# One small maximum moved from the last chunk of a weight-generation loop to behind the last lags

## The chip, the cores and the metric

The kernel runs on one core of a Trainium2 chip. A core has five engines with a queue each: PE (TensorE, matrix products, with its weight loads shown as PEld), DVE (VectorE), ACT (ScalarE), POOL (GpSimd) and SP (SyncE, which here issues most DMAs). The metric is the device time of one execution in microseconds; lower is better. An engine works through its queue in order and waits for other engines by semaphores.

## The reference

Four layers are applied to x of shape (1, 2048, 512): S4 convolution, SwiGLU FFN, and both again with the same weights. Each adds its result to x and starts from a layer norm of x.

```
def A(u):                      # S4
    logdA = exp(log_dt)[:, None] * (A_re + 1j * A_im)          # (512, 128)
    K = einsum("dn,dnl,dn->dl", C, exp(logdA * l), dt * B).real  # 512 kernels of length 2048
    return irfft(rfft(pad(u)) * rfft(pad(K))) + u * Dskip      # causal convolution
def B(x):                      # F = 1376
    return (silu(x @ w_gate) * (x @ w_up)) @ w_down
x = x + A(layernorm(x)); x = x + B(layernorm(x))
x = x + A(layernorm(x)); x = x + B(layernorm(x))
```

## The kernel before, in words

**The generation of the convolution kernels.** The 512 channels are worked through in eight chunks of 64 (`DC`, `NCH`). For each chunk DVE, ACT and POOL build tables of powers (`gen_exp`, `gen_turns`, `gen_trig`, `gen_g` at L454 to L487, `gen_e` at L439 to L452); PE multiplies them into the kernel's lags (`lags`, L489 to L498); ACT copies the lags out (`spread_in`, L507); they are spread over the partitions by DMA, or for the last two chunks by PE (`spread_pe`, L518 to L525); the skip weight is added (`skip`, L503); and PE transforms them to spectra (`spectra`, products in L531, copies in L554 to L559, one sum in L563).

**The scales of the FFN's weights.** The FFN multiplies in fp16, with each weight split into a high and a low half. The scales of the split come from bounds on the weights: `norms` (L314 to L340) loads `w_down`, `w_gate` and `w_up` piece by piece in 43 units and five groups. A unit's ACT instruction squares the piece (L333), and a PE product with a matrix of ones adds the squares of each column into the group's PSUM tile `nrm` (L336). When a group is complete, DVE takes the maximum over its columns (`largest`, L339) into the group's column of `cmx`. `scales` (L342 to L356) makes the maximum of `cmx` (L344) and ten tiny DVE steps of bit arithmetic into `sc6`. ACT needs `sc6` for the first high halves (L664), DVE for the low halves (L669), the FFN for its activations (L915, L916, L929).

**How the order is set.** Up to line 1213 the queues of ACT, DVE, PE and POOL follow the program's order. The chunk loop's order is a hand-written plan: `at(t, f)` enters a step with a due time, the plan is sorted, and the steps are issued one after the other. SP's queue is planned, save in two inner blocks where the plan's steps are issued and SP too follows the program. From line 1214 on, where the FFN begins, all queues are ordered at compile time by a planner that works with costs of its own.

A unit of `norms` goes through the plan in four steps, entered by `weights` (L1075 to L1091): at `t0` the pieces are loaded, at `t1` ACT squares them, at `t2` PE adds them up, and a complete group's maximum goes on the list `tops`, and at `t3` everything on `tops` is taken:

```
            def largest():
                while tops:
                    tops.pop(0)()
            at(t0, lambda: us.extend(u for u in (next(nrm, None) for _ in range(n)) if u))
            at(t1, lambda: [u[0]() for u in us])
            at(t2, product)
            at(t3, largest)
```

The last three units, which complete the fifth group, belong to the chunk of index 6 (`NCH - 2`), which starts at 177 in the plan; their times are set apart in L1104 and L1105 (15.0, 20.0, 24.0 and 27.0 after the chunk's start). The plan's last step is issued in L1130.

**Behind the plan** come the last chunk's lags (L1143), the copy of them (L1157), the first step of the first block's convolution (`take(conv[0], 1)`, L1162: spectrum product L776, sums L781 and L782, inverse transform on PE in L796, copy on ACT in L748), the spreading of the last chunk on PE (L1163), `skip` (L1164), a second step of the convolution (L1165), and then `scales()` (L1166). From there on the split of the weights (`split`), steps of the convolution (L756, L757, L811 to L827), the last spectra (`first_parts`, L580 and L581; `later_parts`, L598 to L600) and the first row statistics and transposes (`first_norm`, L830 to L849, with `stats` in L196 to L210) alternate, until the FFN's first products (L909 to L912) begin.

Small PSUM tiles share four buffers of one tag (`psml`): the tiles `nrm`, the outputs of the second block's transform (`pf`) and those of the inverse transform (`pi`).

**The FFN and the rest.** For each block of 512 rows, PE makes gate and up in fp16 in three products each (L909, L910, L912), ACT and DVE make the SwiGLU of them (L915 to L918), and PE the down product (L924 to L926). Between these, the planner places the convolution of the next block: forward transform (L280), spectrum products and sums on DVE (L776, L779), inverse transform (L796).

Of the kernel before, what the change touches and what calls it, by code (L numbers as in the profile page):

```python
# [74 lines left out]
def kernel(ctx, tc, x, a_re, a_im, b_re, b_im, c_re, c_im, log_dt, d_skip,  # L75
# [266 lines left out]
    def scales():  # L342
        c2 = sb.tile([P, 3], F32, name="c2")
        V.tensor_reduce(c2, cmx, axis=AX.X, op=OP.max)  # L344
        V.tensor_scalar(c2, c2, 1.01, None, OP.mult)
        ex = sb.tile([P, 3], I32, name="ex")
        V.tensor_scalar(ex, c2.bitcast(I32), 23, None, OP.logical_shift_right)
        V.tensor_scalar(ex, ex, 67, -125, OP.max, OP.add)
        V.tensor_scalar(ex, ex, 1, None, OP.arith_shift_right)
        bits = sb.tile([P, 6], I32, name="bits")  # L350
        V.tensor_scalar(bits[:, 0:3], ex, -1, 141, OP.mult, OP.add)
        V.tensor_scalar(bits[:, 3:4], ex[:, 0:1], 1, 105, OP.mult, OP.add)
        V.tensor_scalar(bits[:, 4:5], ex[:, 0:1], -1, 111, OP.mult, OP.add)
        V.tensor_tensor(bits[:, 5:6], ex[:, 0:1], ex[:, 1:2], OP.add)
        V.scalar_tensor_tensor(bits[:, 5:6], bits[:, 5:6], 107, ex[:, 2:3], OP.add, OP.add)
        V.tensor_scalar(sc6.bitcast(I32), bits, 23, None, OP.logical_shift_left)  # L356
# [143 lines left out]
    def skip(ch, kt, eng):  # L500

        k = kt[0:1, :, 0]
        eng.tensor_tensor(k, k, dsk[:, ch * DC:(ch + 1) * DC].rearrange("p (g d) -> p g d", g=4), OP.add)  # L503
# [125 lines left out]
    def take(it, n):  # L629
        for _ in range(n):  # L630
            next(it, None)
# [307 lines left out]
    prods, tops = [], []  # L939
# [11 lines left out]
    with tc.manual_schedule(engines={mybir.EngineType.Activation, mybir.EngineType.DVE, mybir.EngineType.PE, mybir.EngineType.Pool}):  # L951
# [56 lines left out]
        def at(t, f, n=1):  # L1008
            plan.append((t, len(plan), (lambda: take(f, n)) if hasattr(f, "__next__") else f))
# [5 lines left out]
        def prepare(c, t):  # L1015

            def tiles():
                ts[c] = gen_tiles(c)
            at(t + 0.05, tiles)
            steps = {k: later(lambda g=g: g(c, ts[c])) for k, g in  # L1020
                     (("turns", gen_turns), ("exp", gen_exp))}
            tr = later(lambda: gen_trig(ts[c]))
            at(t + 0.35, steps["turns"])
            at(t + 0.45, tr)
            at(t + 13.0, steps["turns"], 3)
            at(t + 13.2, steps["turns"], 3)
            at(t + 17.0, tr)
            at(t + 8.3, steps["exp"], 100)

        def factors(c, t):  # L1030

            at(t + 0.2, lambda: upper(ts[c]))

            def tiles(c):
                gs[c] = tl([P, 2, 32, DC], "g", ("ga", "gb")[c % 2])
            if c == 1:
                at(t + 0.1, lambda: tiles(c))
            if c + 1 < NCH:
                at(t + 8.05, lambda: tiles(c + 1))
            gg, ge = later(lambda: gen_g(c, ts[c], gs[c])), later(lambda: gen_e(ts[c]))  # L1040
            for k in range(4):
                at(t + 0.2 + 2 * k, gg, 2)
            at(t + 0.3, ge)
            for k in range(5):
                at(t + 8.2 + k, gg)
            for k in range(4):
                at(t + 22.0 + 0.6 * k, ge, 1 if k < 3 else 100)

        def use(c, t):

            box, kt, n = {}, kt2[:, c % 2], starts[c + 1]

            def copy():
                box["ks"] = spread_in(box["pk"])
                if c < NCH - 2:
                    spread(c, box["ks"], kt)
            at(t, lambda: box.update(pk=lags(ts[c], gs[c])))
            at(t + 7.1, copy)
            if c == NCH - 2:
                at(t + 10.0, lambda: spread_pe(box["ks"], kt))  # L1060
            at(t + 13.1, lambda: skip(c, kt, V))
            at(t + 25.0, lambda: sizes(c, kt, box["ks"]))
            for q0, ats in list(enumerate(((t + 17.5, t + 25.2, n + 2.1, n + 7.5),
                                      (n + 6.9, n + 14.0, n + 17.3, n + 21.0))))[:2 if c < NCH - 2 else 1]:
                sp = later(lambda q0=q0: spectra(c, kt, q0))
                for t0 in ats:
                    at(t0, sp)

        def second_block(k, t):
            box = []  # L1070
            at(t - 3.0, lambda: box.append(second(*sec[k])))
            at(t + 14.0, lambda: take(box[0], 1))
            at(t + 17.6, lambda: take(box[0], 1))

        def weights(n, t0, t1, t2, t3):  # L1075

            us = []

            def product():
                for s, p, m in us:  # L1080
                    p()
                    if m:
                        tops.append(m)
# [4 lines that stand above are left out]
            at(t0, lambda: us.extend(u for u in (next(nrm, None) for _ in range(n)) if u))  # L1088
            at(t1, lambda: [u[0]() for u in us])
            at(t2, product)  # L1090
            at(t3, largest)  # L1091

        starts = [0.0, 31.0, 62.0] + [93.0 + 28.0 * k for k in range(NCH)]
        for i in range(NCH - 1):
            t = starts[i]
            use(i, t)
            factors(i + 1, t)
            second_block(i, t)
            if i + 2 < NCH:
                prepare(i + 2, t)  # L1100
            for k, t0, t1, t2, t3 in ((0, -13.0, 0.25, 13.9, 22.3), (1, 0.3, 14.5, 17.45, 22.9),
                                      (2, 15.0, 26.5, 28.05, 36.0)):
                n = ((3, 3, 0), (3, 3, 0), (3, 3, 0), (3, 2, 0), (3, 2, 0), (3, 3, 0), (3, 3, 3))[i][k]
                if i == NCH - 2 and k == 2:  # L1104
                    t0, t1, t2, t3 = 15.0, 20.0, 24.0, 27.0  # L1105
                if n:
                    weights(n, t + t0, t + t1, t + t2, t + t3)
        t = starts[NCH - 1]
        late = starts[NCH - 2] + 12.0
        plan.sort()  # L1110
# [23 lines left out]
        def split(hi, lo, load=0):  # L1134
            for _ in range(load):
                loads.pop(0)()
            for _ in range(hi):
                his.pop(0)()
            for _ in range(lo):
                los.pop(0)()  # L1140
# [22 lines left out]
        spread_pe(ks, kts[1])  # L1163
        skip(c, kts[1], V)  # L1164
        take(conv[0], 1)  # L1165
        scales()  # L1166
        split(1, 0)
        first_parts(c, 0)
# [98 lines left out]
```

## Time and profile before

| | |
|---|---|
| median of three runs | 1165.2 us (1164.25 to 1166.44) |
| the profiled execution | 1164.2 us |
| its span, from the first to the last instruction | 1162.0 us |
| its granted TensorE clock | 0.989 of full speed |
| DMA | 150.38 MB, mean 129 GB/s |

"Busy" is the time in which an engine works on an instruction. A line such as "DVE L339" is the engine and the line of the kernel whose instruction it is. Behind a row of the timeline stands in brackets how long the engine was idle before it, and what ended the wait. A row of stages gives for a window of time each engine's busy time and number of instructions, then the granted clock, the DMA engines' busy share and their rate. The chain of waits is followed back from the last instruction: at each step to what released it.

### The profile page before, as it was taken

The page shows a single profiled execution, that of the slowest core. Times are in us where ns is not written, and L with a number is a line of the kernel's source. Part 1 is how long each engine was busy: PE and PEld are TensorE (multiplying, and loading weights), DVE is VectorE, ACT ScalarE, POOL GpSimd, SP SyncE. Part 2 cuts the span into 40 slices and gives each one's busy share as a digit, 9 for nine tenths or more (in the row PEclk, how much of TensorE's full clock was granted, in tenths as well). Part 3 has the DMA queues.
Part 4 walks back from the last instruction along what each step waited for, and adds up shares of the span by engine and source line. Part 5 has one row for each costly group of instructions (what it writes and reads, how often), then busy time and mean ns, then how long its engine had stood idle before and what let it go on. Part 6 is the DMA issues. An engine that isn't in the chain of part 4 may idle for free.

```text
span 1162.0 us, 24400 instructions
## 1 busy us (share of the span) xinstructions
PE 1100.7 (95%) x9942; PEld 877.9 (76%) x9942; DVE 998.6 (86%) x1586; ACT 598.7 (52%) x1198; POOL 107.9 (9%) x162
## 2 busy tenths in 40 slices
PE   2989999998889999999999999999999999999998
PEld 1868888877766868687868687868777686876875
DVE  8999999959789899999899999989994999983212
ACT  6989889733553353557453534655433452334211
POOL 0113222210000010010010000210000010000000
PEclk9989999998899999999999999999999999999999
DMA  5357777866383446332254544343534145312000
GB/s 208 131 161 164 169 175 187 197 171 218 122 268 122 132 122 219 101 115 73 79 155 140 126 162 141 105 128 93 158 109 150 48 122 145 115 42 46 15 23 19
DMA packets 127314, 150.38 MB, mean 129 GB/s; under 512 B 50897, under 2 KB 75985, under 8 KB 127202
## 3 DMA queue, kind: packets, MB, share of 16 engines
q1 hardware_dynamic: 115298, 123.32, 34.8%
q0 software_dynamic: 11904, 25.50, 9.5%
q8 instruction: 78, 1.28, 0.5%
q14 instruction: 34, 0.28, 0.1%
HBM read 98.70 MB, written 33.82 MB: 114 GB/s over the span
## 4 chain that ended last, share of the span: by engine, by line
PE 33%; DVE 27%; issue 7%; DMA 4%; ACT 3%; SPq 1%; POOL 1%; DVEq 0%; ACTq 0%; POOLq 0%
PE pgu L909 5%; PE pgu L910 5%; PE pgu L912 5%; DVE t L776 4%; PE py L924 4%; DVE yk L779 4%; PE py L925 4%; PE py L926 3%; DVE yk L776 3%; DVE z L228 2%; PE pi L796 2%; PE pf L280 2%; DVE sg L916 2%; DMA w<-wdr 2%; DMA mix<-nn 2%
## 5 line engine op out<-in xcount | busy, mean ns | idle before, releaser
L909 PE MATMUL pgu<-mix,wsl 128*128 128x256 f16 x1280 | 299.2, 273 | 5.0 <-DVE sg L916 5.0
L910 PE MATMUL pgu<-mix,wsl 128*128 128x256 f16 x1280 | 298.9, 273 | 0.0
L912 PE MATMUL pgu<-mix,wsl 128*128 128x256 f16 x1280 | 195.4, 273 | 0.0
L910 PEld LDWEIGHTS <-wsl 128*128 128x128 f16 x1280 | 125.4, 98 | 21.9 <-issue 5.4
L924 PE MATMUL py<-wsl,hh 128*128 128x512 f16 (+1 forms) x352 | 133.5, 379 | 6.3 <-DVE xg L929 4.2
L909 PEld LDWEIGHTS <-wsl 128*128 128x128 f16 x1280 | 125.4, 98 | 16.2
L912 PEld LDWEIGHTS <-wsl 128*128 128x128 f16 x1280 | 125.4, 98 | 14.9
L926 PE MATMUL py<-wsl,hl 128*128 128x512 f16 (+1 forms) x352 | 133.4, 379 | 1.2 <-DVE hl L918 1.1
L776 DVE TENSOR_TENSOR t<-uu,w 128x1024 f32<-128x1024 f32 x96 | 116.7, 1215 | 5.5 <-DMA w<-wdr 5.2
L925 PE MATMUL py<-wsl,hh 128*128 128x512 f16 x320 | 121.3, 379 | 0.0
L915 ACT ACTIVATE sg<-pgu,sc 128x512 f32<-128x512 f32 x80 | 54.6, 683 | 126.6 <-PE pgu L912 122.0
L779 DVE TENSOR_TENSOR yk<-yk,t 128x1024 f32<-128x1024 f32 x96 | 116.6, 1214 | 0.1
L916 DVE SCALAR_TENSOR_TENSOR sg<-pgu,sc,sg 128x512 f32<-128x512 f32 x80 | 59.4, 743 | 52.2 <-ACT sg L915 52.0
L917 ACT ACTIVATE hh<-sg 128x512 f16<-128x512 f32 x80 | 50.1, 626 | 82.3 <-DVE sg L916 82.3
L531 PE MATMUL pw<-kt,ek 128*128 128x256 f32 (+1 forms) x384 | 92.2, 377 | 0.0
L531 PEld LDWEIGHTS pw<-kt,ek 128*128 128x128 f32 x384 | 73.5, 196 | 8.7
L796 PE MATMUL pi<-yl,mix 128*128 128x256 f16 x576 | 78.9, 273 | 1.3 <-ACT yl L785 0.9
L280 PE MATMUL pf<-z,eh 128*128 128x256 f16 x576 | 74.9, 272 | 0.6 <-DVE z L228 0.6
L776 DVE TENSOR_TENSOR yk<-u,w0r 128x1024 f32<-128x1024 f32 x56 | 68.0, 1214 | 0.8 <-ACT u L282 0.8
L918 DVE TENSOR_TENSOR hl<-sg,hh 128x512 f16<-128x512 f32 x80 | 54.7, 683 | 15.5 <-ACT hh L917 15.5
L496 PE MATMUL pk<-re,g 128*32 128x64 f32 x1024 | 65.1, 317 | 2.6 <-DMA g<-g 1.9
L925 PEld LDWEIGHTS <-hh 128*128 128x128 f16 (+1 forms) x352 | 34.5, 98 | 42.5 <-issue 7.0
(237 smaller groups left out, 2160.5 us busy)
## 6 DMA issues: line engine op xcount, KB each, us to landing
w<-wdr SPq DMA_DIRECT2D x96, 256.0 KB, 2.8
uu<-udr SPq DMA_DIRECT2D x96, 256.0 KB, 3.0
udr<-u POOLq DMA_DIRECT2D x32, 256.0 KB, 2.6
g<-g POOLq DMA_DIRECT2D x6, 1024.0 KB, 9.1
udr<-u SPq DMA_DIRECT2D x16, 256.0 KB, 2.9
n<-xdr SPq DMA_DIRECT2D x4, 1024.0 KB, 5.7
kdr<-ks SPq DMA_DIRECT2D x6, 512.0 KB, 2.6
kt<-kdr SPq DMA_DIRECT2D x24, 128.0 KB, 3.0
```

The costliest lines, as they stand in the source:

```text
L280: PE.matmul(pf[:, o], lhsT=e, rhs=m, start=k == 0, stop=k == len(terms) - 1)
L531: PE.matmul(pw[:, i], lhsT=e, rhs=kt[:, :, c + 4 * k0:4 * k1:4, :].rearrange("p g k d -> p k g d"), start=c == 0, stop=c == 3)
L776: V.tensor_tensor(t, uu.unsqueeze(2).to_broadcast([P, NQ, 2, 2, DC]), w.unsqueeze(3).to_broadcast([P, NQ, 2, 2, DC]), OP.mult)
L779: V.tensor_tensor(yk, yk, t, OP.add)
L796: PE.matmul(pi[:, o], lhsT=e, rhs=m, start=k == 0, stop=k == len(terms) - 1)
L909: PE.matmul(o, lhsT=wgu(wi, k, 0)[:, fs], rhs=nh[:, k], start=k == 0, stop=False)
L910: PE.matmul(o, lhsT=wgu(wi, k, 1)[:, fs], rhs=nh[:, k], start=False, stop=False)
L912: PE.matmul(o, lhsT=wgu(wi, k, 0)[:, fs], rhs=nlo[:, k], start=False, stop=k == 3)
L916: V.scalar_tensor_tensor(sg, pgu[:, 1], sc6[:, 4:5], sg, OP.mult, OP.mult)
L924: PE.matmul(py[:, r], lhsT=hh[:n, f, rc], rhs=wd(f, 0)[:n], start=f == 0, stop=False)
L925: PE.matmul(py[:, r], lhsT=hh[:n, f, rc], rhs=wd(f, 1)[:n], start=False, stop=False)
L926: PE.matmul(py[:, r], lhsT=hl[:n, f, rc], rhs=wd(f, 0)[:n], start=False, stop=f == FT - 1)
```

## The change

The maximum of the last group is no longer entered in the plan: its `t3` is `None`, and `weights` then leaves the step out. In its place whatever is still on `tops` is taken right before `scales()`, behind `skip` and the second step of the convolution. That is one DVE instruction (L339) on one group of columns; the four other maxima stay where they are.

```diff
             at(t2, product)
-            at(t3, largest)
+            if t3:
+                at(t3, largest)
...
                 if i == NCH - 2 and k == 2:
-                    t0, t1, t2, t3 = 15.0, 20.0, 24.0, 27.0
+                    t0, t1, t2, t3 = 15.0, 20.0, 24.0, None
                 if n:
-                    weights(n, t + t0, t + t1, t + t2, t + t3)
+                    weights(n, t + t0, t + t1, t + t2, t3 and t + t3)
...
         take(conv[0], 1)
+        while tops:
+            tops.pop(0)()
         scales()
         split(1, 0)
```

## The prediction

> **What bounds the kernel now.** I read the page first: the busy shares, then the chain that ended last.
>
> ```profile
> span 1162.0 us, 24400 instructions
> PE 1100.7 (95%) x9942; PEld 877.9 (76%) x9942; DVE 998.6 (86%) x1586; ACT 598.7 (52%) x1198; POOL 107.9 (9%) x162
> PE 33%; DVE 27%; issue 7%; DMA 4%; ACT 3%; SPq 1%; POOL 1%; DVEq 0%; ACTq 0%; POOLq 0%
> ```
>
> TensorE has 95% of the span and VectorE (DVE) 86%, but the averages do not say what one moved DVE instruction costs. The change touches two places some 15 us apart, so I asked for the timeline around each. First the old place, engine by engine:
>
> ```profile
> 245.29 1.17 DVE L451 TENSOR_TENSOR re<-re,mu 128x992 f32<-128x992 f32 x1
> 248.41 0.52 DVE L339 TENSOR_REDUCE cmx<-nrm 128x1 f32<-128x344 f32 x1 [1.94 <-PE nrm L336]
> 249.22 0.99 DVE L563 TENSOR_TENSOR wo<-pw,wo 128x768 f32<-128x768 f32 x1 [0.30 <-ACT w0r L559]
> 250.12 1.23 DVE L776 TENSOR_TENSOR yk<-mix,w0r 128x1024 f32<-128x1024 f32 x1
> 251.74 0.42 DVE L782 TENSOR_TENSOR yf<-yk 128x256 f32<-128x256 f32 x1
> ...
> 246.47 1.46 PE L531 MATMUL pw<-kt,ek 128*128 128x256 f32 x6
> 247.77 0.60 PE L336 MATMUL nrm<-sq,onesb 128*128 128x344 bf16 x3
> 248.30 0.49 PE L496 MATMUL pk<-re,g 128*32 128x64 f32 x8
> ...
> 246.78 1.04 ACT L607 ACTIVATE ks<-kt 128x1024 f32<-128x1024 f32 x1
> 247.97 0.92 ACT L554 ACTIVATE wo<-pw 128x384 f32<-128x384 f32 x2
> 248.76 0.43 ACT L559 ACTIVATE w0r<-pw 128x256 f32<-128x256 f32 x1
> ```
>
> The columns are start, duration, engine, line, operation, and in brackets the idle time before it with its releaser. The maximum (L339) makes DVE wait 1.94 us for the column sums (L336), which PE makes only behind the products of L531. It ends at 248.41 + 0.52 = 248.93. The next DVE instruction, L563, does not start there: it waits another 0.30 us for ACT, whose L559 ends at 248.76 + 0.43 = 249.19. So the wait for the maximum is covered by a later one.
>
> Then the new place:
>
> ```profile
> core 0: us, PE busy (x) PEld busy (x) DVE busy (x) ACT busy (x) POOL busy (x), PEclk, DMA share, GB/s
> 261.60:299.00 37.40, 28.34 (x152) 24.93 (x152) 36.10 (x69) 10.69 (x18) 1.35 (x1) 0.88 0.58 193
> ...
> 261.63 0.21 DVE L503 TENSOR_TENSOR kt<-kt,tdk 1x64 f32<-1x64 f32 x1 [9.47 <-ACT kt L525]
> 263.36 0.42 DVE L782 TENSOR_TENSOR yf<-yk 128x256 f32<-128x256 f32 x1
> 263.69 0.15 DVE L344 TENSOR_REDUCE c<-cmx 128x3 f32<-128x6 f32 x1
> 263.88 0.17 DVE L345 TENSOR_SCALAR c<-c 128x3 f32<-128x3 f32 x1
> 265.27 0.17 DVE L356 TENSOR_SCALAR sc<-bits 128x6 int32<-128x6 int32 x1
> 265.52 1.44 ACT L664 ACTIVATE wsl<-st,sc 128x1376 f16<-128x1376 f32 x1 [3.92 <-DVE sc L356]
> ```
>
> Between the places DVE has 9.47 us of idle time, which the lags on PE and two copies on ACT end (L525). From 261.63 on it is the bound: it is busy 36.10 of 37.40 us, while PE has 28.34 and ACT 10.69. The rest of DVE's time is the few hundredths between dependent instructions. The chain of waits in this stage and the next shows where that stretch hands over:
>
> ```profile
> 296.95 1.58 DVE wsl L669 x2
> 298.64 0.16 DVE rs L209
> 298.83 0.82 ACT nn L841
> 299.70 0.48 PE pt L843
> 301.67 11.62 PE pw L531 x64
> 315.02 5.24 DMA st<-in_B_w_down_dram
> ```
>
> L209 is the last step of the first row statistics. PE's transposes follow it, and behind them the last weight-spectrum products and the first matmuls of the FFN. So what is added to DVE between 261.63 and 298.64 is added to the start of the FFN.
>
> **The change, part by part.**
>
> *What is taken away at 248.41.* One reduce of 0.52 us and its wait of 1.94 us. L563 then waits directly for L559 and starts at 249.22, as now: gain 0.00. The bounds: nothing below zero, since an instruction leaves; at most 0.30 us if the wait for L559 is really one for L554, which ends at 247.97 + 0.92 = 248.89. Even that would go into the 9.47 us of idle time in front of L503, behind which only L525 decides. PE's lags (L496, 248.30) start before the reduce does and do not wait for it. I take 0.
>
> *What is added at 263.69.* The same reduce, between L782 and L344. Its input has long been there, so it waits for nothing; its own size is read from its two last calls:
>
> ```profile
> 241.63 0.50 DVE L339 TENSOR_REDUCE cmx<-nrm 128x1 f32<-128x344 f32 x1
> 242.06 2.20 DVE L448 SCALAR_TENSOR_TENSOR im<-im,mu 128x1984 f32<-128x1984 f32 x1
> ```
>
> Where the next instruction does not need its result, it follows 0.43 us after the reduce's start (242.06 − 241.63). Here the next one, L344, reads what it writes. L345 shows what a dependent successor costs: it starts 0.19 us after L344's start, which lasts 0.15, so 0.04 us more than the duration. The reduce is then worth 0.50 + 0.04 = 0.54 us; bounds 0.43 and 0.56. I take 0.54, because the dependence is there in the code. Queued behind it are L344 to L356, then every DVE instruction of the stretch; waiting for L356 is ACT's L664, now 3.92 us, then 4.46. ACT has 10.69 us of work in 37.40, so its own queue takes this up.
>
> *The bank of column sums.* The PSUM tile of the last group is given back at 264.2 instead of 248.9. Four buffers share its tag. In that time only two outputs of the inverse transform (pi) ask for one, and the tile of the second block is free by then: three free ones for two askers, so nothing waits. If one had to wait nevertheless, it would be the second, until 263.69 + 0.54 = 264.23 instead of 263.50:
>
> ```profile
> 263.50 3.43 PE L796 MATMUL pi<-yf,mix 128*128 128x256 f32 x8 [2.98 <-DVE yf L781]
> ```
>
> That is 0.7 us on PE, which has 37.40 − 28.34 = 9.1 us to spare in the stretch; I take 0. No DMA is issued by the moved step, and no queue of SP or POOL holds anything for it.
>
> *The sum.* 0.00 + 0.54 = +0.54 us at L209. Behind 299.70 the chain is PE work and transfers that it releases, so they start as much later. What follows is PE:
>
> ```profile
> 317.00:1162.00 845.00, 824.76 (x6879) 636.61 (x6876) 709.76 (x1175) 366.18 (x706) 53.67 (x69) 1.00 0.38 114
> PE pgu L909 <- DVE sg L916: 5.0, 3, 4.5
> L776 DVE TENSOR_TENSOR t<-uu,w 128x1024 f32<-128x1024 f32 x96 | 116.7, 1215 | 5.5 <-DMA w<-wdr 5.2
> ```
>
> PE is busy 824.76 of 845.00 us there, so there is little room to lose the 0.54 in, and it passes to the end. The profiled execution took 1164.2 us (its span of 1162.0 and 2.2 around it): 1164.2 + 0.54 = 1164.7. The median of the three runs is 1165.2, 1.0 above that execution; on the median the forecast is 1165.2 + 0.5 = **1165.7 us**. That is 0.05% and far inside 0.2% (2.33 us), about what a measurement of this kernel can tell from no change.
>
> *The clock.* The stages with PE pauses show one more thing:
>
> ```profile
> 281.00:283.50 2.50, 0.00 (x0) 0.00 (x0) 2.43 (x5) 0.00 (x0) 0.00 (x0) 1.00 0.28 102
> 283.50:286.60 3.10, 3.09 (x7) 2.52 (x8) 3.10 (x4) 0.00 (x0) 0.00 (x0) 0.50 0.00 0
> 286.60:289.20 2.60, 2.57 (x11) 1.78 (x10) 2.50 (x6) 1.99 (x3) 0.00 (x0) 0.94 0.92 270
> 294.40:299.70 5.30, 0.00 (x2) 0.00 (x1) 4.72 (x11) 0.87 (x2) 1.35 (x1) 0.76 0.13 49
> 301.20:303.70 2.50, 2.50 (x10) 2.50 (x9) 0.31 (x1) 2.00 (x6) 0.00 (x0) 0.50 0.83 260
> 303.70:306.00 2.30, 2.30 (x15) 2.30 (x15) 0.24 (x1) 1.61 (x6) 0.00 (x0) 0.94 0.28 86
> ```
>
> The last figure but two is the granted clock. If it is always 0.5 or 1, the shares place the switches: down at 283.50, up 0.31 us into the third row (286.91); down 2.54 us before 299.70 (297.16), up 0.28 us into the last (303.98). The distances are 3.41, 10.25 and 6.82 us, that is 1, 3 and 2 times 3.41: the switches lie on a fixed grid and not at the starts of the work. In this execution PE works at half clock from 299.70 to 303.98, 4.28 us, which costs 2.14. Start it 0.54 us later on the same grid, and it is 3.74 us and 1.87: 0.27 of the 0.54 comes back. In other executions the grid lies elsewhere, and one step more or less at half clock is 3.41 / 2 = 1.7 us. I keep 0.54 as the mean, and 1.7 each way for the range. [...]
>
> **The rivals.**
>
> *1. The planner orders the rest anew, for the better.* Up to the FFN, DVE, ACT, PE and POOL follow the program's order. Behind it the order comes from planned times, and a step moved by half a microsecond can turn pairs around. For it: DVE is busy 709.76 of 845.00 us beside PE's 824.76, so the order of L776 against L916 matters. Against it: the whole plan shifts together. A price: the longest single wait of PE for L916 is 4.5 us; without it, 1165.7 − 4.5 = 1161.2.
>
> *2. The same, for the worse (the other side).* Place: DVE's queue behind 317, where L916 must free a gate-and-up bank for PE. If instructions of the long convolution (L776, 1.215 us each) get in front of an L916 for which PE then waits, as once already, one more such wait gives 1165.7 + 4.5 = 1170.2. It decides from a net 2.33 − 0.54 = 1.8 us, two such instructions at a place where PE has no other work.
>
> *3. The clock's grid.* The mechanism above, when the executions timed fall otherwise on it: 1164.0 to 1167.4. Within 0.2% at both ends.
>
> *4. The removed wait reaches the end.* Then 1.94 us goes and 0.54 comes: 1165.2 − 1.4 = 1163.8. Against it stand L559 and the 9.47 us.
>
> **How the numbers follow.** The forecast has 0.43, rival 3 0.10 and rival 4 0.03; all three are within 0.2%: same 0.56. Rival 1 has 0.20 (faster), rival 2 0.24 (slower); a little more than rival 1, because the 0.54 counts on its side. The range: around 1165.7, the two ends of the clock reach 1164.0 and 1167.4, and the executions before spread by 1.1 us (1164.25 to 1166.44). The planner's cases have 0.44 together, so the range must take in more than half of them to leave out no more than 2 in 10: it ends just past both of their prices, 1161.0 to 1170.5. The likeliest case's own range is 1164.0 to 1167.4.
>
> **What would show it.** In the profile of the changed kernel: L339 between L782 and L344, without an idle time, 0.50 us long; L563 waiting for L559 with about 2.75 us of idle time (0.30 + 0.52 + 1.94) instead of 0.30; still over 9 us in front of L503; L356 and L209 0.54 us later against L503; the first matmul of L909 as much later. The forecast is wrong if L503 moves, if DVE shows a pause between L503 and L209 that takes up the reduce, or if DVE's or PE's order behind the first L909 differs and PE's idle time there moves by over 2 us from 20.2.

## The result and the profile after

The changed kernel takes 1163.0 us (median of 10 runs, 1161.51 to 1164.28), the kernel before beside it 1165.2 us (10 runs, 1164.25 to 1167.99). The ratio is 0.9978, with a 95% interval of 0.9968 to 0.9988: faster by 1.4 to 3.7 us. In a second comparison it took 1163.8 us against 1164.45, a ratio of 0.9989 (0.9980 to 0.9998); one execution there of the kernel before, of 2884 us, is left out as slow. So there is a gain, between 0.2 and 3.7 us by the two, where 0.5 us more had been forecast.

The page of the changed kernel's profiled execution begins with the span and the busy shares:

```profile
span 1160.5 us, 24403 instructions
PE 1102.5 (95%) x9942; PEld 878.4 (76%) x9942; DVE 998.6 (86%) x1586; ACT 599.3 (52%) x1198; POOL 109.2 (9%) x162
```

Its own time is 1162.8 us. The shares do not show the gain: DVE's busy time is the same to the tenth. The timeline of the changed kernel shows both places of the move (start, duration, engine, line, operation, idle time before it and its releaser):

```profile
243.92 2.28 DVE L451 TENSOR_TENSOR re<-re,mu 128x992 f32<-128x992 f32 x2
249.15 0.96 DVE L563 TENSOR_TENSOR wo<-pw,wo 128x768 f32<-128x768 f32 x1 [2.95 <-ACT w0r L559]
...
261.58 0.21 DVE L503 TENSOR_TENSOR kt<-kt,tdk 1x64 f32<-1x64 f32 x1 [9.53 <-ACT kt L525]
...
263.64 0.51 DVE L339 TENSOR_REDUCE cmx<-nrm 128x1 f32<-128x344 f32 x1
264.18 0.16 DVE L344 TENSOR_REDUCE c<-cmx 128x3 f32<-128x6 f32 x1
...
299.16 0.15 DVE L209 SCALAR_TENSOR_TENSOR rs<-mv,rs 128x2 f32<-128x2 f32 x1
...
266.02 1.44 ACT L664 ACTIVATE wsl<-st,sc 128x1376 f16<-128x1376 f32 x1 [4.48 <-DVE sc L356]
```

Up to here it went as worked out. L563 waits 2.95 us for L559 and starts where it did (249.15, before 249.22). L503 has 9.53 us of idle time in front. The reduce costs 264.18 − 263.64 = 0.54 us. From L503 to L209 it takes 299.16 − 261.58 = 37.58 us, before 298.64 − 261.63 = 37.01: 0.57 us more.

The difference lies behind the FFN's start. The timeline of the kernel before at 370 us:

```profile
370.56 1.22 DVE L776 TENSOR_TENSOR yk<-u,w0r 128x1024 f32<-128x1024 f32 x1
371.70 1.22 DVE L776 TENSOR_TENSOR t<-uu,w 128x1024 f32<-128x1024 f32 x1
372.83 0.74 DVE L929 SCALAR_TENSOR_TENSOR xg<-py,sc,xg 128x512 f32<-128x512 f32 x1
...
373.63 0.38 PE L924 MATMUL py<-wsl,hh 128*128 128x512 f16 x1 [1.18 <-DVE xg L929]
```

And that of the changed kernel at the same work:

```profile
371.60 1.22 DVE L776 TENSOR_TENSOR yk<-u,w0r 128x1024 f32<-128x1024 f32 x1
372.74 0.74 DVE L929 SCALAR_TENSOR_TENSOR xg<-py,sc,xg 128x512 f32<-128x512 f32 x1
373.40 1.22 DVE L776 TENSOR_TENSOR t<-uu,w 128x1024 f32<-128x1024 f32 x1
...
373.24 0.21 PE L877 MATMUL pgu<-wsl,mix 128*128 128x96 f16 x1
373.53 0.38 PE L924 MATMUL py<-wsl,hh 128*128 128x512 f16 x1
```

The residual sum (L929), which empties the PSUM tile of the down product for PE's next one, has changed places with the second spectrum product (L776). Before, PE waits 1.18 us for it; now it does not wait. It starts 1.14 us behind the first L776 (372.74 − 371.60) instead of 2.27 (372.83 − 370.56), because an instruction of 1.22 us that used to be ahead of it is now behind it.

This is no slip of one execution: the queues themselves differ. Up to the FFN all five engines have the same instructions in the same order, save the reduce. Behind it DVE's queue differs in 42 lines at 20 places, all between the 491st and the 580th of its 1586 busy instructions; ACT's and SP's differ in 8 lines each. PE's products interleave a little differently in that stretch, POOL's queue is the same, and from about 420 us on the order is the old one again. The planner has turned pairs around in one short stretch.

PE's waits between 366 and 424 us (what waited for what: us in total, times, longest), kernel before:

```profile
PE py L924 <- DVE xg L929: 1.2, 1, 1.2
PE py L926 <- DVE hl L918: 1.1, 1, 1.1
```

And the changed kernel:

```profile
PE py L926 <- DVE hl L918: 1.0, 2, 0.5
```

The wait for L929 is gone; that for the low halves (L918) is halved at one place and has a small copy at another.

### The profile page after: what moved, and what is told of

Same layout as the page of the kernel before. It is cut to its first block, busy times and chain, and to the rows that moved or that the text cites. A ratio compares the mean times of both kernels' runs of the same rounds, so it can differ in the third digit from the quotient of the medians.

```text
span 1160.5 us, 24403 instructions
## 1 busy us (share of the span) xinstructions
PE 1102.5 (95%) x9942; PEld 878.4 (76%) x9942; DVE 998.6 (86%) x1586; ACT 599.3 (52%) x1198; POOL 109.2 (9%) x162
## 3 DMA queue, kind: packets, MB, share of 16 engines
q8 instruction: 78, 1.28, 0.5%
## 4 chain that ended last, share of the span: by engine, by line
DVE 29%; PE 29%; issue 8%; DMA 5%; ACT 3%; SPq 1%; POOL 1%; DVEq 0%; ACTq 0%; POOLq 0%
PE pgu L909 5%; PE pgu L910 5%; PE pgu L912 5%; DVE t L776 5%; DVE yk L779 4%; PE py L924 3%; PE py L925 3%; PE py L926 3%; DVE yk L776 3%; DVE z L228 3%; PE pi L796 2%; DMA w<-wdr 2%; DVE sg L916 2%; PE pf L280 2%; DVE hl L918 2%
## 5 line engine op out<-in xcount | busy, mean ns | idle before, releaser
L909 PE MATMUL pgu<-mix,wsl 128*128 128x256 f16 x1280 | 300.0, 274 | 6.3 <-DVE sg L916 5.2
L924 PE MATMUL py<-wsl,hh 128*128 128x512 f16 (+1 forms) x352 | 133.4, 379 | 4.7 <-DVE xg L929 3.0
L909 PEld LDWEIGHTS <-wsl 128*128 128x128 f16 x1280 | 125.6, 98 | 16.2
L776 DVE TENSOR_TENSOR t<-uu,w 128x1024 f32<-128x1024 f32 x96 | 117.0, 1219 | 4.6 <-DMA w<-wdr 4.4
L916 DVE SCALAR_TENSOR_TENSOR sg<-pgu,sc,sg 128x512 f32<-128x512 f32 x80 | 59.8, 747 | 52.1 <-ACT sg L915 51.9
L796 PE MATMUL pi<-yl,mix 128*128 128x256 f16 x576 | 78.9, 272 | 0.6 <-DVE yl L228 0.3
L776 DVE TENSOR_TENSOR yk<-u,w0r 128x1024 f32<-128x1024 f32 x56 | 68.3, 1219 | 0.8 <-ACT u L282 0.8
L918 DVE TENSOR_TENSOR hl<-sg,hh 128x512 f16<-128x512 f32 x80 | 55.0, 687 | 15.5 <-ACT hh L917 15.4
```

The lines of the kernel that those rows point to most:

```text
L776: V.tensor_tensor(t, uu.unsqueeze(2).to_broadcast([P, NQ, 2, 2, DC]), w.unsqueeze(3).to_broadcast([P, NQ, 2, 2, DC]), OP.mult)
L796: PE.matmul(pi[:, o], lhsT=e, rhs=m, start=k == 0, stop=k == len(terms) - 1)
L909: PE.matmul(o, lhsT=wgu(wi, k, 0)[:, fs], rhs=nh[:, k], start=k == 0, stop=False)
L916: V.scalar_tensor_tensor(sg, pgu[:, 1], sc6[:, 4:5], sg, OP.mult, OP.mult)
L924: PE.matmul(py[:, r], lhsT=hh[:n, f, rc], rhs=wd(f, 0)[:n], start=f == 0, stop=False)
```

## The experiments

Three theories stood against each other. **Order**: the planner's other order behind the FFN's start makes the gain, and the reduce at its new place costs 0.5 us of it. **Wait**: the removed wait of 1.94 us at 248.41 reaches the end (rival 4). **Stray**: executions differ by more than the effect, for reasons outside the kernel. The experiments ran in three series, each on one chip, with the kernel before beside them: it took 1164.4 us in the first (1 to 4, median of 35), 1164.45 in the second (5 to 8, 25) and 1163.9 in the third (9 to 11, 23).

**1. The order alone.** The reduce stays at its old place; an instruction of one column, which nothing reads, stands at the new one. All queues save PE's interleaving then have the changed kernel's order:

```diff
         take(conv[0], 1)
+        nj = sb.tile([P, 4], F32, name="nj")
+        V.tensor_scalar(nj[:, :1], mhalf[:, :1], 1.0, None, OP.mult)
         scales()
```

> The kernel before, with one tiny DVE instruction (one column, read by nobody) in front of scales(); the maximum stays at its old place with its wait. From the FFN on the queues of DVE, ACT, POOL and SP stand in the changed kernel's order. Theory 'order' (the planned order behind the FFN's start is worth about 2.7 us, the maximum at its new place costs 0.5): 1165.2 - 2.7 + 0.1 = 1162.6 us, ratio 0.998. Rival 'wait' (taking the maximum and its wait away from the old place brings the gain, wherever it goes): 1165.3, ratio 1.000. Rival 'stray' (the gain is spread between executions and the place of the clock's grid): 1164 to 1165.2, nothing clear.

The timeline of this kernel shows what the added instruction costs, start to start: 0.06 us.

```profile
263.84 0.14 DVE L1167 TENSOR_SCALAR nj<-mhalf 128x1 f32<-128x1 f32 x1
263.90 0.15 DVE L344 TENSOR_REDUCE c<-cmx 128x3 f32<-128x6 f32 x1
```

Measured: 1162.65 us, ratio 0.9985 (0.9977 to 0.9994). An instruction of 0.06 us, added for nothing, makes the kernel 1.8 us faster by the medians (0.7 to 2.7 by the interval). The removed wait is still there, so it is not what makes the gain.

**2. The move alone.** The reduce is taken out of the plan as in the change, but issued in DVE's 9.5 us of idle time, in front of the spreading of the last chunk. The order stays that of the kernel before:

```diff
         take(conv[0], 1)
+        while tops:
+            tops.pop(0)()
         spread_pe(ks, kts[1])
```

> The maximum moved behind the last lags too, but into DVE's idle time in front of the spreading of the last chunk; all queues behind it stand in the order of the kernel before. 'Order': 1165.2 us, ratio 1.000, since neither the order changes nor the dense stretch grows. 'Wait': 1165.2 - 2.7 = 1162.5, ratio 0.998. 'Stray': nothing clear.

Measured: 1164.3 us, ratio 1.0000 (0.9991 to 1.0009). The wait at 248.41 is gone and the time is the same within 1.0 us either way; the wait theory expected 2.7 us less. Against the wait theory this is the cleanest run.

**3. Both places.** The reduce stays at its old place and is repeated at the new one; the order is exactly the changed kernel's.

```diff
-        plan = []
+        plan, again = [], []
...
-                    tops.pop(0)()
+                    again[:] = [tops.pop(0)]
+                    again[0]()
...
         take(conv[0], 1)
+        again.pop()()
         scales()
```

> The maximum is taken at its old place, with its wait, and once more at the new place; every other instruction of all five queues stands as in the changed kernel. 'Order': the changed kernel's time, 1163.0 us, ratio 0.998; against the kernel with the tiny instruction it shows the price of the maximum in the dense stretch, +0.5 us. 'Wait': 1165.2 + 0.5 = 1165.7, ratio 1.000. 'Stray': nothing clear.

Measured: 1163.8 us, ratio 0.9990 (0.9982 to 0.9999): the change's own gain, with the old wait kept.

**4. The move and the order.** The reduce in the idle time (as in 2) and the instruction of one column at the new place (as in 1).

> The maximum in DVE's idle time, and one tiny DVE instruction (one column, read by nobody) in front of scales(), so that the queues of DVE, ACT, POOL and SP stand in the changed kernel's order without the 0.5 us of the maximum in the dense stretch. 'Order': 1162.6 us, as with the tiny instruction alone, and 0.5 below the changed kernel. 'Wait': 1162.6 as well, but then the move alone has it too. 'Stray': nothing clear.

Measured: 1162.8 us, ratio 0.9985 (0.9976 to 0.9993). It is the version with the order's gain and without the reduce's price; a second run follows below.

Of each of these kernels' traces I took the starts of the same PE instruction and subtracted those in the trace of before. How that difference changes over the stretch in question:

| kernel | order | difference at 370 us | at 424 us | change |
|---|---|---|---|---|
| the changed kernel | new | +1.04 | −0.48 | −1.52 |
| 1, order alone | new | +1.28 | −0.27 | −1.55 |
| 2, move alone | old | −0.01 | +0.18 | +0.19 |
| 3, both places | new | −0.09 | −1.71 | −1.62 |
| 4, move and order | new | +0.59 | −0.95 | −1.54 |

The differences at 370 us, between −0.1 and +1.3, are each execution's own: between 330 and 338 us, for one, the granted clock is 0.79 in the profile of before and 0.57 in that of the changed kernel. The step of 1.5 us hardly varies, and only the new order has it. Of it, 1.13 us come at 373.6 (the wait for L929) and 0.63 at 422, where L918 ends earlier:

```profile
422.00 0.68 DVE L918 TENSOR_TENSOR hl<-sg,hh 128x512 f16<-128x512 f32 x1
...
422.74 0.39 PE L926 MATMUL py<-wsl,hl 128*128 128x512 f16 x1 [1.07 <-DVE hl L918]
```

This was the kernel before, and these are the rows of the changed kernel:

```profile
421.52 0.69 DVE L918 TENSOR_TENSOR hl<-sg,hh 128x512 f16<-128x512 f32 x1
...
422.26 0.39 PE L926 MATMUL py<-wsl,hl 128*128 128x512 f16 x1 [0.48 <-DVE hl L918]
```

Some 0.24 us are given back between, where PE's own products stand in another order. The stages from 366 to 424 us say the same of PE's total. Kernel before, then the move alone, then the changed kernel (length, then busy time and number of instructions of PE, PEld, DVE, ACT, POOL, then clock, DMA share, GB/s):

```profile
366.00:424.00 58.00, 55.60 (x439) 42.02 (x438) 54.48 (x107) 29.10 (x60) 5.08 (x6) 1.00 0.39 117
```

```profile
366.00:424.00 58.00, 55.09 (x435) 41.63 (x433) 54.19 (x107) 28.88 (x60) 5.07 (x6) 1.00 0.38 117
```

```profile
366.00:424.00 58.00, 56.88 (x448) 42.62 (x447) 55.83 (x108) 29.70 (x60) 5.92 (x6) 1.00 0.40 122
```

PE has 1.3 to 1.8 us more work done in the same 58 us; with the order alone (1) it is 56.88 as well.

**5. The changed kernel again**, to size the change.

> The changed kernel once more, beside the kernel before on one chip, to size the change. By the order theory it is the sum of two terms that the traces show: 1.5 us less between 366 and 395 us from the new order, 0.5 us more from the reduce in the dense stretch, together 1.0 less: 1163.4 if the kernel before takes 1164.4. If the first comparison's difference of 2.2 us comes back (1162.2), the two terms are not all of it, and most of the reduce's 0.5 us must have been absorbed by the clock's grid or something else be shorter. By the stray theory (executions differ for reasons outside the kernel) it lies within 0.5 us of the kernel before.

Measured: 1163.8 us, ratio 0.9989 (0.9980 to 0.9998): −0.7 us by medians, −1.3 by the ratio, around the −1.0 of the sum. The step from 370 to 424 us is again 0.75 to −0.78 = −1.53. Its profiled execution, though, has a span of 1162.0 us, exactly that of before: one pair of profiles would have shown no gain at all. Part of what executions add is a transfer in front of L878. PE's waits of the first profile of the changed kernel have this row,

```profile
PE pgu L878 <- DMA mix<-nn: 0.4, 1, 0.4
```

and those of the second this one, as before the change:

```profile
PE pgu L878 <- DMA mix<-nn: 1.0, 1, 1.0
```

**6. The reduce three times**, at the new place. Save the two added reduces, the queues of DVE, ACT, POOL and SP are the changed kernel's.

```diff
-        while tops:
-            tops.pop(0)()
+        last = tops.pop()
+        for _ in range(3):
+            last()
         scales()
```

> The changed kernel with the moved reduce issued three times in a row at its new place; the queues of all engines are otherwise those of the changed kernel. It tells whether time added to DVE there reaches the end. By the prediction's step (what is added between 261.63 and 298.64 passes to the end) two more reduces of 0.43 to 0.54 us each cost 0.9 to 1.1 us against the changed kernel of this call: about 1164.4 if that takes 1163.4. If the clock's grid takes up half of such delays, 0.5 us; if a wait behind the stretch takes them up, nothing.

Measured: 1164.8 us, ratio 1.0002 (0.9994 to 1.0011), 1.0 us above the changed kernel of the same series (1.5 by the ratios, whose intervals still overlap a little). The timeline gives the local price, 265.37 − 263.73 = 1.64 us for three, 0.55 each:

```profile
263.73 1.61 DVE L339 TENSOR_REDUCE cmx<-nrm 128x1 f32<-128x344 f32 x3
265.37 0.16 DVE L344 TENSOR_REDUCE c<-cmx 128x3 f32<-128x6 f32 x1
```

So time added to DVE in the dense stretch does pass to the end, as long as the order stays, and the prediction's own sum holds for a fixed order. Again it takes the medians to see it: the profiled execution of this kernel has a span of 1160.9 us, less than the 1162.0 of run 5.

**7. The residual sum ahead, by hand.** The kernel before, with the one pair set as in the changed kernel (L929 of the first block before the second product of L776). The planner plans what follows anew, and about 300 lines of DVE's queue come out otherwise. Line numbers here are 2 higher at L776 and 4 higher at L909 to L929.

```diff
+    tins = []
...
-                V.tensor_tensor(t, uu..., w..., OP.mult)
+                ti = V.tensor_tensor(t, uu..., w..., OP.mult)
+                if k:
+                    tins.append(ti.ins)
...
-                    V.scalar_tensor_tensor(xt[:, r], py[:, r], sc6[:, 5:6], xt[:, r], OP.mult, OP.add)
+                    li = V.scalar_tensor_tensor(xt[:, r], py[:, r], sc6[:, 5:6], xt[:, r], OP.mult, OP.add)
+                    if ready and c == 0:
+                        tc.add_manual_dep(tins[6], li.ins.name, ...)
```

> The kernel before, the reduce at its old place, with one order set by hand: the first residual sum of the first block of the FFN (L929) ahead of the second product t of the convolution (L776), as in the changed kernel. The planner plans the rest anew around it, so other pairs differ too. By the order theory PE's wait of 1.18 us at 373.6 is gone and the first 1.1 us of the new order's 1.5 appear between 366 and 373 us; the total is open, because the rest of the order differs from both kernels: 1163.3 if the rest costs nothing, up to some 3 us either way if other pairs decide. By the wait theory, in which the removed wait at 248 us makes the gain, nothing changes there: 1164.4.

Measured: 1168.0 us, ratio 1.0026 (1.0016 to 1.0036), 3.5 us slower. The first half of the expectation holds: the difference to before falls from +1.02 at 370 us to −0.12 at 380, by 1.14 us. Then it rises to +5.12 at 395. The timeline of this kernel shows why:

```profile
379.59 1.23 DVE L778 TENSOR_TENSOR yk<-u,w0r 128x1024 f32<-128x1024 f32 x1 [0.27 <-DVE rs L224]
380.74 1.22 DVE L778 TENSOR_TENSOR t<-uu,w 128x1024 f32<-128x1024 f32 x1
381.99 1.23 DVE L783 TENSOR_TENSOR yk<-yk,t 128x1024 f32<-128x1024 f32 x1
383.13 2.09 DVE L228 SCALAR_TENSOR_TENSOR bt<-n 128x256 f32<-128x256 f32 x6
385.14 0.74 DVE L933 SCALAR_TENSOR_TENSOR xg<-py,sc,xg 128x512 f32<-128x512 f32 x1
...
385.94 0.27 PE L913 MATMUL pgu<-mix,wsl 128*128 128x256 f16 x1 [3.30 <-DVE xg L933]
...
386.62 0.42 PE L913 MATMUL pgu<-mix,wsl 128*128 128x256 f16 x1
...
390.22 0.27 PE L913 MATMUL pgu<-mix,wsl 128*128 128x256 f16 x1
```

The next residual sum stands behind nine instructions of the convolution, PE waits 3.30 us for it, and right behind the pause its products take 0.42 us instead of 0.27 from 386.5 to 389.9. The granted clock from 380 to 390 us is 0.83, so 0.17 × 10 = 1.7 us are lost: a step of 3.4 us at half clock. Together that is 5.0 of the 5.24. It is rival 2, at L929 instead of L916.

**8. The residual sum behind, by hand.** The changed kernel with the same pair set as in the kernel before; DVE's queue differs from the changed kernel's in some 800 lines.

```diff
-                    V.scalar_tensor_tensor(xt[:, r], py[:, r], sc6[:, 5:6], xt[:, r], OP.mult, OP.add)
+                    with tc.issue_after(tins[6]) if ready and c == 0 else ExitStack():
+                        V.scalar_tensor_tensor(xt[:, r], py[:, r], sc6[:, 5:6], xt[:, r], OP.mult, OP.add)
```

> The changed kernel with the opposite order set by hand: the same residual sum (L929) not before the second product t (L776), as in the kernel before. The planner plans the rest anew. By the order theory PE waits again about 1.2 us for the sum near 373 us and the first 1.1 us of the gain is lost locally: 1164.5 or more if the changed kernel takes 1163.4, with some 3 us either way for the other pairs. By the wait theory it keeps the changed kernel's time.

Measured: 1173.7 us, ratio 1.0071 (1.0058 to 1.0083). The wait is back as expected (in this kernel L924 is L928 and L929 is L934):

```profile
375.72 0.38 PE L928 MATMUL py<-wsl,hh 128*128 128x512 f16 x1 [1.18 <-DVE xg L934]
```

The step of −1.13 us is missing: the difference to before is +2.09 at 370 and at 380 us. So one pair, turned either way by hand, makes or takes 1.1 us at its place; but the 9.3 us of the total come from the rest of the order.

**9. The reduce four times.** One more than in 6, and the planner flips again: save the three added reduces, the queues of DVE, ACT, POOL and SP are now those of 8.

> The changed kernel with the moved reduce issued four times in a row, one more than in the run with three. With the fourth, the planner's order behind the first matmuls of the FFN becomes, on DVE, ACT, POOL and SP, that of the run with the residual sum set behind (which took 1173.7 us); only the three added reduces differ from it. By the order theory the time is set by that order: 1173.7 plus three reduces at about 0.5 us, 1175.2, and PE shows the same waits. If time on DVE passed on to the end were all (the prediction's step), it would be half a microsecond above the run with three (1164.8): 1165.3. So a fourth reduce costs about 10 us or about 0.5.

Measured: 1173.2 us, ratio 1.0077 (1.0065 to 1.0089). Three reduces gave 1164.8 in the second series; the fourth, 0.55 us of DVE, costs over 8 us. That is 2 us below the 1175.2 expected of the order, and 8 above the 1165.3 of the local sum. The rows of this kernel's PE waits behind 317 us that differ most from before,

```profile
PE py L924 <- DVE xg L929: 6.8, 6, 2.3
...
PE py L924 <- DVE xf L929: 3.2, 3, 2.3
```

against 4.2 and 1.6 us in the same rows of the kernel before, make 4.2 us of the 10.7 by which its span is longer. Behind one of the two longest the clock falls, and it falls again behind two shorter waits at 880 us, as the timeline and then the stages show:

```profile
485.88 1.22 DVE L776 TENSOR_TENSOR t<-uu,w 128x1024 f32<-128x1024 f32 x1
487.02 0.74 DVE L929 SCALAR_TENSOR_TENSOR xg<-py,sc,xg 128x512 f32<-128x512 f32 x1
...
487.82 0.38 PE L924 MATMUL py<-wsl,hh 128*128 128x512 f16 x1 [2.27 <-DVE xg L929]
...
660.70 0.38 PE L924 MATMUL py<-wsl,hh 128*128 128x512 f16 x1 [2.35 <-DVE xf L929]
...
879.81 0.27 PE L796 MATMUL pi<-yl,mix 128*128 128x256 f16 x1 [1.21 <-ACT yl L785]
880.85 0.38 PE L924 MATMUL py<-wsl,hh 128*128 128x512 f16 x1 [0.78 <-DVE xg L929]
```

```profile
480.00:490.00 10.00, 7.73 (x81) 5.11 (x79) 9.73 (x17) 7.37 (x17) 2.30 (x2) 0.95 0.41 123
490.00:500.00 10.00, 10.00 (x57) 5.80 (x56) 9.91 (x18) 2.40 (x4) 0.00 (x0) 0.88 0.23 68
655.00:665.00 10.00, 7.65 (x49) 4.04 (x47) 10.00 (x18) 4.54 (x12) 0.00 (x0) 1.00 0.40 123
880.00:890.00 10.00, 9.22 (x42) 4.33 (x41) 9.24 (x13) 1.38 (x4) 0.00 (x0) 0.83 0.46 137
```

The missing clock, (0.05 + 0.12) × 10 = 1.7 us, is one step at half clock, and the 0.17 × 10 = 1.7 us of the last row are a second one. The remaining 3.1 us were not followed row by row.

**10. One line up.** The reduce between the adding of the skip weight and the second step of the convolution, still in the dense stretch; about 300 lines of DVE's queue differ from the kernel before.

> The changed kernel with the reduce one step earlier, between the adding of the skip weight and the second step of the convolution: the same dense stretch, the same 0.5 us. Its planned order behind the FFN's start is another one again (some 150 lines of DVE's queue stand elsewhere than in the kernel before). By the prediction's step the place inside the stretch does not matter and it takes what the kernel before takes and 0.5 us more: 1164.9. By the order theory the time is that of its own order, which the traces at hand do not show: of the three orders timed beside that of the kernel before, one was 1.8 us faster, one 3.5 and one 9.3 us slower, so most likely 1 to 9 us slower than before, and over 2.3 us away from 1164.9.

Measured: 1162.8 us (1162.05 to 1169.08), ratio 0.9994 (0.9983 to 1.0005). The expectation of 1 to 9 us more was wrong: this order is no worse than that of before, and by its median as good as the new one. Its range of 7 us is wider than that of the others, and the interval leaves open whether it gains. What can be said is that a different order need not cost, and that its price could not be read off beforehand.

**11. The version of 4 again.**

> Once more the version with the changed kernel's order and the reduce in DVE's idle time (an instruction of one column stands at the new place, so that the planner's order is the changed kernel's). By the order theory it keeps the 1.5 us of the order and pays the 0.06 us of the small instruction: 1162.9 if the kernel before takes 1164.4, as in its first run (1162.8). If the gain was chance it comes out at 1164.4.

Measured: 1162.5 us, ratio 0.9991 (0.9983 to 1.0000), the step from +0.52 to −1.01 = −1.53 again. In its two series its median was the lowest but one and the lowest (1162.8 and 1162.5, against 1163.0 and 1163.8 of the changed kernel). It is the version to keep, though against the changed kernel its 0.5 us is not shown by a comparison on one chip.

## Why the prediction was wrong

**The old place: right.** Gain 0.00 forecast; the move alone (2) measured 1.0000, and with it rival 4, the removed wait that reaches the end, is out.

**The new place: right.** 0.54 forecast, 0.54 start to start, 0.57 at L209, 0.55 each for three. **Its way to the end: right for a fixed order.** Two more reduces cost 1.0 to 1.5 us in the total. The bank of column sums and ACT's queue also held: the second inverse transform (L796) starts at 263.44, before at 263.50, and L664 waited 4.48 us, 4.46 forecast.

**The clock's grid: right in kind, larger in this execution.** 0.27 us of the 0.54 were to come back. In the stages of the changed kernel behind L843, which now starts at 300.22,

```profile
300.16:303.70 3.54, 3.48 (x15) 3.48 (x16) 0.00 (x0) 2.19 (x7) 0.00 (x0) 0.57 0.91 236
303.70:306.00 2.30, 2.30 (x16) 2.30 (x15) 0.56 (x1) 2.24 (x8) 0.00 (x0) 1.00 0.35 109
```

the clock is up again before 303.70: 0.43 × 3.54 × 2 = 3.0 us at half clock, against 4.28, so 0.6 us came back, and the first L909 starts at 316.46, before at 316.57, where it had been forecast 0.54 us later. The repeated run began the FFN 0.43 us later than before, and the run with three reduces 0.92: it is luck of the execution, not a gain.

**The order: here it failed.** The failing step is the sentence against rival 1, "the whole plan shifts together". On it the forecast got 0.43 and rival 1 only 0.20. In the runs the plan did not shift together. An instruction of 0.06 us turned some 40 lines of DVE's queue over 100 us later, and this is worth −1.5 us; with the reduce's 0.54 the sum is −1.0. Rival 1 happened, though not as it was priced: the wait of 4.5 us for L916 stayed (4.7 in the changed kernel), and what went was 1.18 us for L929 and 0.6 for L918. The prediction's own sign of this came true: the order behind the first L909 differs, and PE's idle time there fell from 20.2 to 17.8 us. The orders timed here are worth from about −1.5 to +9 us, so the bound of 4.5 for rival 2 was too small as well.

**The size.** The repeated run and the run with both places lie at −1.3 and −1.2 us by their ratios, which fits −1.0. The first comparison, −2.2 with an interval of −3.7 to −1.4, lies below it; the kernel before took 0.8 us more in those ten runs than in the 60 of the two series that followed. The spread of 1.1 us that the prediction gives for the kernel before is half of what its two ends make (1166.44 − 1164.25 = 2.19 us), and the ten runs spread by 3.7. No run shows a third cause, and whether that excess is more than chance stays open. Also open is why the planner flips: only its result, the order, was seen.

## What to carry to other kernels

Where queues are ordered by a planner at compile time, an edit has two prices: its own, worked out from the rows around it, and that of the order that it tips over, which may lie 100 us behind it and be many times larger. Compare the instruction order of the two programs before adding up a sum; where it differs, the local sum holds only for the part up to the first difference. To separate the two on the chip, add an instruction that does nothing at the place of the edit, and make the edit where the order stays: here 1.8 us and 0.0.

## What was not expected of the hardware

A pause of PE shorter than a step of the clock's grid (3.41 us) cost a whole step at one place and nothing at another: in run 9 the clock fell to a half for one step behind 2.27 us of waiting at 487.82, 1.7 us, while behind 2.35 us at 660.70 it did not.

The place on the grid can be worked out. In the profile of the kernel before the granted clock is 0.53 from 263.0 to 263.5 us and 0.80 from 331.0 to 331.5; taken as falls from 1 to 0.5 these lie at 263.03 and 331.30, 20 steps of 3.413 us apart. In run 9 the products of the down projection start 0.215 us apart up to 488.89, 0.25 from there to 489.14 and then 0.43, so the fall lies at 489.07. The step that ends there holds 2.2 us of the pause before 487.82. Counted on by the same 3.413 us, an edge at 659.7 splits the pause before 660.70 into 1.4 and 1.0 us, and the step that ends at 881.6 holds the two pauses of 1.21 and 0.78 us, with a step of half clock in the 0.83 of 880 to 890 us.

The same wait of L796 for L781 in the two profiles shows it once more. Before, PE is idle for 2.98 us in front of 263.50, 2.5 of them in the step that ends at 263.03, and the clock falls there. In the changed kernel it is idle for 2.99 us in front of 263.44; its clock is 0.54 from 330.5 to 331.0 us, a fall at 330.54, and 20 steps ahead of that an edge at 262.3 splits the pause into 1.8 and 1.2 us: the clock is 1.00 from 262 to 267 us. The price of such a fall stands in run 7: 3.30 us of waiting and 1.7 of half clock behind it are 5.0 of the 5.24 us lost there. How much idle time in a step brings the fall is not shown in general.
